# One PSUM copy for both heads, 128-column key transposes, a table row spread by TensorE, and a new order

## The chip, the core and the metric

The kernel runs on one core of a Trainium2 chip. The metric is device time in microseconds (us) of one execution; the profile of one such execution gives its span, from the first instruction to the last, and every instruction in it. Engines are TensorE (PE in the rows; PEld is its weight load), VectorE (DVE), ScalarE (ACT), GpSimd (POOL) and SyncE (SP, which here issues nearly all DMAs).

## What is computed

Attention with a learned bias by relative position, whose output goes through a feed-forward block. q, k and v are (4, 8, 576, 64), the hidden width of the bias network is 32, the feed-forward sizes are 512 and 2048, all in fp32.

```python
scores = scale * np.matmul(q, k.transpose(0, 1, 3, 2))
psi_rel = np.log1p(np.abs(rel))                       # rel[i, j] = i - j
psi_i = np.log1p(np.maximum(pos[:, None], 1.0))
x = (psi_rel / psi_i)[..., None]
h = np.maximum(x @ w1 + b1, 0.0)
bias = h @ w2                                         # one value per head
attn = softmax(scores + bias)                         # over the last axis
x = np.matmul(attn, v)                                # heads side by side: (2304, 512)
h = x @ w_in
g = h * (1.0 / (1.0 + np.exp(-1.702 * h)))
return g @ w_out
```

## The kernel before

**Tiling.** The attention is cut into units (`units`): a batch, a chunk of 128 query rows and a pair of heads. For a unit `scores` (L946) multiplies on TensorE into PSUM, `reduce` (L955, VectorE) adds the bias and takes the extreme of each row, `expo` (L964, ScalarE) takes exponentials and their row sums, `inverse` (L971, L973) inverts the sums. From the ninth unit on, the scaled exponentials are split into a high and a low 16-bit half (`exp_hi`, L991 on VectorE or L993 on ScalarE; `exp_lo`, L734 by way of `lo_part`), turned by a DMA, and multiplied with the values in `av` (L1063). The first eight units (`DIRECT = 8`) go another way: `diagonal` (L1004) makes a diagonal matrix of the inverses, `turn_pe` (L1012, L1017) turns and scales the fp32 exponentials of one head with five TensorE matmuls into the PSUM tile `op` (one bank for each head) and an `hp` tile, `turn_out` (L1022 on ScalarE, L1024 on VectorE) copies 128x512 of one head to SBUF, `turn_tail` (L1028) copies the rest, and `av_direct` (L1039) multiplies in fp32.

**Bias.** One row of distances is broadcast by a DMA to 128 partitions (`load_tab`, L580) and scaled by two engines (L569, L576). `relu` (L621 on ScalarE, L623 on VectorE) makes the hidden layer, `products` (L647) multiplies it with w2, `bias_evict` (L659, L661) leaves PSUM, and the rows go to DRAM and come back skewed, one load for each pair of heads.

**Keys.** For batches 0 and 1 (four groups of four heads) `load_k` (L798) brings a group in with one DMA, `trans_k` (L826) transposes it with 22 fp32 matmuls against the identity into the four-bank PSUM tile `sp`, ScalarE (L892) and VectorE (L734) split it. For batches 2 and 3 a DMA transposes.

**Feed-forward.** Weights come as pairs of 32-bit words of 64-bit floats; `merge` (L1197, L1201, L1205, VectorE) builds fp32, `w_split` (L1221 on ScalarE or L1223 on VectorE, then L734) makes 16-bit halves. For each of nine blocks of 256 rows and 16 slices `m1` (L1274) and `m2` (L1312) multiply; between them stand `tanh` (L1282), `gate_mul` (L1288), `gate_hi` (L1296 on ScalarE, L1298 on VectorE) and `gate_lo` (L1303, VectorE or GpSimd). `out_evict` (L1320, L1322) and `out_store` (L1332) end a block.

**Order.** Nothing in the code's sequence sets the order. Each step is a task with an engine, a duration, dependences, buffers and a priority; the class `Plan` plays the engines through and lists the tasks as they start. `TURNS` holds one priority for each task, `WHERE` names the engine of the tasks that have a choice (A ScalarE, V VectorE, P GpSimd), `SLACK` is added to each DMA's landing, `COLD` stretches TensorE's durations in a window, and `WARM` puts warming matmuls (L1369, 256 columns, output not used) ahead of numbered TensorE tasks. Every engine then runs its list strictly in that order.

## Time and profile before

| | |
|---|---|
| median of 3 runs | 656.45 us (654.28 to 656.5) |
| the profiled execution | 655.45 us |
| its span | 653.7 us |
| mean granted TensorE clock | 0.988 of full |
| busy: TensorE, VectorE, ScalarE, GpSimd | 607.3, 521.2, 370.8, 66.7 us |
| DMA | 113.91 MB, mean 174 GB/s |

A stage's busy times say which engine is full there. The chain of waits is followed back from the last instruction: each piece is the work that released the next. An engine that is full and holds most of the chain sets the stage. A granted clock of 1.00 is 2.4 GHz, 0.50 is 1.2 GHz.

### The profile page before, as it was taken

To read this page: it belongs to the slowest core of one execution; us is meant where nothing else is said; L and a number is where in the kernel's file an instruction comes from. 1 tells how busy PE (TensorE), PEld (TensorE's weight loads), DVE (VectorE), ACT (ScalarE), POOL (GpSimd) and SP (SyncE) were. 2 spreads that over 40 slices of the span, in tenths; PEclk is the share of its full clock that TensorE was granted. 3 is DMA by queue.
4 is the path that set the end of the run, shared out by engine and by line. 5 is a ranking of instruction groups with operands and counts; after the bars stand their busy time and mean duration, and the time that the engine had idled before them with its cause. 6 is when DMAs were issued, how large, how long until landed. Compare 5 with 4: busy or idle time off the path is not lost.

```text
span 653.7 us, 22298 instructions
## 1 busy us (share of the span) xinstructions
PE 607.3 (93%) x9485; PEld 433.5 (66%) x9485; DVE 521.2 (80%) x1377; ACT 370.8 (57%) x831; POOL 66.7 (10%) x101
## 2 busy tenths in 40 slices
PE   5769999988799999999899989999999999999997
PEld 2446776656565676766676657766777677767874
DVE  6996988999999979989479967977875793995322
ACT  4884577987886765556345545745434661661311
POOL 3000000121121000001011100110001200110111
PEclk9988999999999999999999989999999999999999
DMA  9997587599998799999999988979844983375000
GB/s 218 289 306 226 147 235 226 132 259 216 251 260 191 152 237 183 195 181 201 200 210 209 244 185 115 198 116 241 171 75 107 182 149 97 74 118 103 34 3 33
DMA packets 254915, 113.91 MB, mean 174 GB/s; under 512 B 233952, under 2 KB 234592, under 8 KB 254816
## 3 DMA queue, kind: packets, MB, share of 16 engines
q1 hardware_dynamic: 252192, 107.94, 78.5%
q10 hardware_dynamic: 2624, 4.55, 2.1%
q8 instruction: 74, 1.21, 0.8%
q14 instruction: 25, 0.20, 0.1%
HBM read 52.55 MB, written 15.61 MB: 104 GB/s over the span
## 4 chain that ended last, share of the span: by engine, by line
PE 63%; DVE 24%; ACT 4%; DMA 4%; issue 4%; ACTq 1%; SPq 0%; POOL 0%; DVEq 0%; POOLq 0%
PE op L1312 21%; PE hp L1274 20%; PE sp L946 6%; PE hp L1063 6%; DVE wide L734 5%; DVE wide L955 4%; PE sp L826 3%; PE op L1017 2%; DVE narrow L1201 2%; DVE th L1288 2%; DVE narrow L1205 2%; DVE w L734 2%; PE hp L1039 1%; ACT wide L964 1%; DMA wide<-in_k_dram 1%
## 5 line engine op out<-in xcount | busy, mean ns | idle before, releaser
L1274 PE MATMUL hp<-xT,w 128*64 128x256 f16 x3456 | 204.8, 273 | 4.7 <-DVE th L1288 2.8
L1312 PE MATMUL op<-w,gT 128*64 128x512 f16 x1728 | 203.2, 382 | 2.0 <-POOL gT L1303 1.3
L1274 PEld LDWEIGHTS <-w 128*64 128x64 f16 x3456 | 186.5, 110 | 24.5 <-issue 16.1
L964 ACT ACTIVATE wide<-wide,sm 128x576 f32<-128x576 f32 x144 | 110.8, 770 | 68.7 <-DVE sm L955 68.2
L1312 PEld LDWEIGHTS <-gT 128*64 128x64 f16 x1728 | 97.0, 110 | 79.5 <-issue 6.5
L1303 POOL TENSOR_TENSOR gT<-th,gT 128x256 f16<-128x256 f32 x80 | 61.7, 773 | 577.2 <-ACT gT L1296 341.9
L955 DVE CUSTOM_DVE_ANT_0 wide<-sp,wide 128x576 f32<-128x576 f32 x144 | 104.8, 752 | 7.3 <-PE sp L946 7.1
L734 DVE SCALAR_TENSOR_TENSOR wide<-wide,sm,wide 128x576 f16<-128x576 f32 x128 | 105.3, 841 | 5.2 <-ACT wide L993 4.8
L1282 ACT ACTIVATE th<-hp 128x256 f32<-128x256 f32 x144 | 53.7, 376 | 79.7 <-PE hp L1274 57.3
L1288 DVE SCALAR_TENSOR_TENSOR th<-th,hp 128x256 f32<-128x256 f32 x144 | 59.3, 416 | 48.8 <-ACT th L1282 48.2
L946 PE MATMUL sp<-wide,narrow 64*128 64x512 f16 (+2 forms) x720 | 65.5, 320 | 9.0 <-DVE sm L955 4.5
L1063 PE MATMUL hp<-wide,v 128*64 128x128 f16 (+1 forms) x2160 | 60.3, 214 | 5.0 <-issue 3.5
L1063 PEld LDWEIGHTS <-v 128*64 128x64 f16 x2160 | 57.7, 111 | 10.9 <-issue 7.0
L946 PEld LDWEIGHTS <-narrow 64*128 64x128 f16 (+1 forms) x960 | 28.8, 97 | 43.9 <-issue 23.8
L621 ACT ACTIVATE wide<-tab,bp 128x496 f32<-128x496 f32 (+17 forms) x94 | 55.4, 650 | 0.4 <-ACT narrow L1320 0.4
L993 ACT ACTIVATE wide<-wide,sm 128x576 f16<-128x576 f32 x63 | 47.2, 767 | 11.5 <-DVE sm L973 7.7
L1296 ACT CAST gT<-th 128x256 f16<-128x256 f32 x80 | 31.9, 400 | 34.7 <-DVE th L1288 21.5
L991 DVE TENSOR_SCALAR wide<-wide,sm 128x576 f16<-128x576 f32 x65 | 34.8, 545 | 0.1
L1303 DVE TENSOR_TENSOR gT<-th,gT 128x256 f16<-128x256 f32 x64 | 26.6, 422 | 4.5 <-ACT gT L1296 3.5
L971 DVE TENSOR_SCALAR sm<-sm 128x1 f32<-128x1 f32 (+1 forms) x128 | 19.9, 158 | 11.6 <-ACT wide L964 11.0
L647 PE MATMUL sp<-wide,pk 128*32 128x512 f32 (+28 forms) x312 | 23.6, 431 | 5.1 <-DVE sm L955 3.5
L964 ACT ACTIVATION_READ_ACCUMULATOR wide<-wide,sm 128x1 f32 x144 | 27.0, 188 | 0.0
(83 smaller groups left out, 513.6 us busy)
## 6 DMA issues: line engine op xcount, KB each, us to landing
wide<-scr SPq DMA_DIRECT2D x32, 576.0 KB, 4.9
scr<-narrow SPq DMA_DIRECT2D x30, 295.5 KB, 4.3
wide<-in_moe_w_in_dram SPq DMA_DIRECT2D x16, 512.0 KB, 6.0
wide<-in_moe_w_out_dram SPq DMA_DIRECT2D x16, 512.0 KB, 5.1
narrow<-in_q_dram SPq DMA_DIRECT2D x16, 256.0 KB, 4.7
out_dram<-narrow ACTq DMA_DIRECT2D x15, 256.0 KB, 2.4
w<-in_v_dram SPq DMA_DIRECT2D x4, 576.0 KB, 8.2
w<-in_k_dram SPq DMA_DIRECT2D x4, 576.0 KB, 6.3
```

What stands on the lines that cost most here:

```text
L621: nc.scalar.activation(out=h, in_=tv, func=ACTF.Relu, bias=bp[:, pb:pb + 1])
L734: nc.vector.scalar_tensor_tensor(out=out, in0=in0, scalar=scale, in1=in1, op0=ALU.mult, op1=ALU.subtract)
L946: nc.tensor.matmul(pair[64 * e:64 * e + m, a, cs], lhsT=qt[r, x, hp + e, q0:q0 + m], rhs=k_of(b, hp + e, y, cs)[r], start=i == 0, stop=i == 2,
L955: nc.vector.tensor_tensor_reduce(out=slot(("a32", u))[:, cs], in0=slot(("sp", u)).rearrange("p (h a) n -> p h (a n)", h=2)[:, a, 0:S], in1 ...
L964: nc.scalar.activation(out=t, in_=t, func=ACTF.Exp, scale=-1.0, bias=sm[:, a:a + 1], accum_out=sm[:, 2 + a:3 + a])
L993: nc.scalar.activation(out=o, in_=t, func=ACTF.Identity, scale=r)
L1063: nc.tensor.matmul(o[64 * a:64 * a + 64, po], lhsT=vt[:, x, vc:vc + 64], rhs=t[:, 9 * y + k0, po], start=kb < 0 and i == 0, stop=kb == 3 a ...
L1274: nc.tensor.matmul(p[y0:y0 + FF, :n], lhsT=wi16[:, f // 4, cc, z, w0:w0 + FF], rhs=r, start=i == 0, stop=i == 11, skip_group_check=FF < 128,)
L1282: nc.scalar.activation(out=slot(("th", j, f))[:, :n], in_=slot(("hp", j, f))[:, :n], func=ACTF.Tanh, scale=0.851 / (XS * WIS))
L1288: nc.vector.scalar_tensor_tensor(out=th, in0=th, scalar=1.0, in1=slot(("hp", j, f))[:, :n], op0=ALU.add, op1=ALU.mult)
L1303: (nc.vector if on("low", NF * j + f) == "V" else nc.gpsimd).tensor_tensor(out=gt[:, 1, :n], in0=th, in1=gt[:, 0, :n], op=ALU.subtract)
L1312: nc.tensor.matmul(o[y0:y0 + FF, i], lhsT=gt[:, z, 128 * i + y0:128 * i + y0 + FF], rhs=wo16[:, NF - 1 - f, y, :], start=f == 0 and n3 == ...
```

## The change

- `turn_out` runs once for a unit, after the second head's turning, and copies both heads' banks (128x2x512) in one instruction; `diagonal` may run on ScalarE (7 of 16 do).
- Keys of batches 0 and 1: two DMAs for a group, each partition holding four neighbouring rows, and the last 64 rows of all heads of both batches by two more DMAs, once. `trans_k` turns two heads at a time, 128 columns in one matmul, into every fourth PSUM column, and the last 64 rows in a matmul of 64 columns: 10 matmuls for 22.
- The distance row is loaded into one partition; `spread_tab` multiplies it with a column of ones into `op` (512 and 64 columns), and the two scaling instructions read it there. The inversion of the bias scale is cut into a first 32 columns and the rest.
- In the last block the second half's result goes to a bank of `sp`, and the last `m2` is cut into its halves, so that each half has its own end.
- The planner: `SLACK` 1500 in place of 2500, plus 1000 after 70 us of planned time; 4% more on VectorE, ScalarE and GpSimd after 100 us; a few durations. New `WHERE`, `TURNS` and `WARM`: 47 warming matmuls in place of 93. In instructions, VectorE's high halves of exponentials go from 65 to 48, its `gate_lo` from 64 to 51 (GpSimd's from 80 to 93), its high halves of weights from 8 to 18. `K_PE` and `Q_PE` are empty sets: their code is not reached.

```diff
-SLACK = 2500
+SLACK = 1500
 COLD = (35000, 120000, 1.1)
+LATER = (70000, 1000)
+SPARE = (100000, 1.04)
...
+                    occ = occ * (SPARE[1] if e in ("DVE", "ACT", "POOL") and now > SPARE[0] else 1)
...
-                        end += SLACK
+                        end += SLACK + (LATER[1] if now > LATER[0] else 0)
...
-        4, 21, 10, 29, 40, 28, 49, 43, 33, 68, 585, 132, 45, 705, 184, 218,
...
-    WARM = {4: 5, 9: 10, 13: 6, 14: 10, 15: 8, 16: 8, 34: 4, 39: 3, 40: 8, 46: 9, 47: 7, 53: 6, 57: 3, 59: 6}
+    WARM = {2: 10, 10: 10, 12: 5, 17: 6, 18: 6, 19: 5, 61: 5}
...
     def load_tab():
-        row = dist[0:1].rearrange("p (f a) -> p f a", f=4)[:, :, PB0:]
         nc.sync.dma_start(
-            out=slot("raw")[:, 0:S].rearrange("p (f a) -> p f a", f=4), in_=row.broadcast_to([128, 4, LPH - PB0])
+            out=slot("raw")[0:1, 0:S].rearrange("p (f a) -> p f a", f=4),
+            in_=dist[0:1].rearrange("p (f a) -> p f a", f=4)[:, :, PB0:],
         )
+    def spread_tab():
+        p = slot("tp").rearrange("p a n -> p (a n)")
+        for x, y in ((0, 512), (512, S)):
+            nc.tensor.matmul(
+                p[:, x:y], lhsT=th_tiles[0][0:1, 0:128], rhs=slot("raw")[0:1, x:y], start=True, stop=True
+            )
...
     def trans_k(b, e):
-        t, pair = slot(("k32", b, e)).rearrange("p (u k d) -> p u k d", u=2, k=9), k_psum(b, e)
+        t, pair = k_in(b, e), k_psum(b, e)
+        tail = slot(("kt", b // 2))[:, 0:512].rearrange("p (u x) -> p u x", u=NP)
         for u in range(2):
-            for c in range(5):
-                for a in range(2):
...
-                            nc.tensor.matmul(
-                                pair[64 * a:64 * a + 64, u, lo:hi], lhsT=t[po, u, 4 * a + c],
-                                rhs=idn[po, po.start + lo - x:po.start + hi - x], start=True, stop=True,
-                            )
+            for c in range(4):
+                nc.tensor.matmul(
+                    pair[:, u, c:SM:4], lhsT=t[:, u, c].rearrange("p a d -> p (a d)"), rhs=idn, start=True, stop=True,
+                )
+            nc.tensor.matmul(
+                pair[:, u, SM:S], lhsT=tail[:, 2 * e + u, :], rhs=idn[:, ST * (b % 2):ST * (b % 2) + ST],
+                start=True, stop=True,
+            )
...
-    def turn_out(u, a):
-        t = slot(("aT", u))[:, 640 * a:640 * a + 512]
-        if on("turn", 3 * u + a) == "A":
-            nc.scalar.copy(t, slot(("pt", u))[:, a])
+    def turn_out(u):
+        t = slot(("aT", u))[:, 0:512]
+        t = bass.AP(t.tensor, t.offset, [t.ap[0], (640, 2), (1, 512)])
+        if on("turn", 3 * u) == "A":
+            nc.scalar.copy(t, slot(("pt", u)))
...
+    def o_of(j, i):
+        return slot(("o2", j))[:, 0] if j == len(blocks) - 1 and i else slot(("op", j))[:, i]
...
+            for parts in [(0,), (1,)] if last and f == NF - 1 else [(0, 1)]:
```

TensorE's list, from the last bias products to the first feed-forward matmul, before (L1369 is a warming matmul, L1039 a direct product, L647 bias products, three more and six more warming matmuls stand on either side):

```order
L1369 MATMUL hp_124<-less 128x256
L1039 MATMUL hp_123<-w_63 64x128 x10
L647 MATMUL sp<-wide_95,pk 32x304 x2
L647 MATMUL sp<-wide_88,pk 32x304 x2
L647 MATMUL sp<-wide_96,pk 32x320 x2
L647 MATMUL sp<-wide_100,pk 32x320 x2
L1369 LDWEIGHTS less
```

The same place after the change (L1083 is the direct product, L666 the bias products, L1318 the first feed-forward matmul's weights):

```order
L1083 MATMUL hp_123<-w_63 64x128 x10
L1083 MATMUL hp_124<-w_63 64x128 x10
L666 MATMUL sp<-wide_88,pk 32x304 x2
L666 MATMUL sp<-wide_99,pk 32x304 x2
L666 MATMUL sp<-wide_86,pk 32x320 x2
L666 MATMUL sp<-wide_89,pk 32x320 x2
L1318 LDWEIGHTS w_63
```

The warming matmuls around the last products are gone, and two direct products stand together ahead of them.

SP's first DMAs before:

```order
L580 DMA w_63<-in_dist_dram 128x4x144
L743 DMA narrow_102<-in_q_dram 128x8x64
L903 DMA w_63<-in_v_dram 128x18x64 x2
L1190 DMA wide_84<-in_moe_w_in_dram 128x1024
L798 DMA w_63<-in_k_dram 128x18x64
```

and after (`in_dist` the distance row, `in_k` first the last 64 rows, then a group's two halves):

```order
L1234 DMA wide_84<-in_moe_w_in_dram 128x1024
L585 DMA w_63<-in_dist_dram 1x4x144
L945 DMA w_63<-in_v_dram 128x18x64
L1234 DMA wide_85<-in_moe_w_out_dram 128x1024
L1234 DMA wide_86<-in_moe_w_out_dram 128x1024
L817 DMA narrow_102<-in_k_dram 64x8x64 x2
L762 DMA narrow_104<-in_q_dram 128x8x64
L825 DMA w_63<-in_k_dram 128x8x64 x2
```

A weight load stands ahead of the distance row now, two more ahead of the first queries, which moved from second place to seventh.

ScalarE's last rows before (`narrow_108` was evicted by VectorE):

```order
L1282 ACTIVATE th_120<-hp_124 128x256
L1282 ACTIVATE th_121<-hp_123 128x256
L1296 CAST gT_118<-th_120 128x256
L1320 ACTIVATE narrow_105<-op 128x512
L1332 DMA out_dram<-narrow_108 128x512
```

and after (L1367 the two evictions, L1379 the first half's store; SP stores the second half):

```order
L1340 CAST gT_118<-th_121 128x256
L1326 ACTIVATE th_120<-hp_123 128x256
L1367 ACTIVATE narrow_105<-op 128x512
L1379 DMA out_dram<-narrow_105 128x512
L1367 ACTIVATE narrow_109<-sp 128x512
```

Both halves are ScalarE's now, from two PSUM tiles, with the first half's store between them.

## Rows read from the trace of the kernel before

**Rows 1.** Busy time of each engine by stage; first the columns, us.

```profile
core 0: us, PE busy (x) PEld busy (x) DVE busy (x) ACT busy (x) POOL busy (x), PEclk, DMA share, GB/s
0.00:47.00 47.00, 29.93 (x419) 17.68 (x419) 39.55 (x87) 32.49 (x57) 4.96 (x21) 0.97 1.01 272
47.00:117.00 70.00, 66.93 (x718) 47.78 (x719) 59.44 (x155) 45.39 (x99) 0.00 (x0) 0.94 0.75 210
117.00:205.00 88.00, 77.04 (x1170) 52.54 (x1170) 87.57 (x204) 72.98 (x166) 15.46 (x19) 1.00 0.90 218
205.00:280.00 75.00, 74.82 (x1200) 51.79 (x1198) 68.70 (x190) 46.59 (x104) 4.02 (x6) 1.00 0.98 195
280.00:380.00 100.00, 91.43 (x1780) 67.30 (x1778) 82.53 (x221) 49.69 (x119) 10.91 (x13) 1.00 1.16 208
380.00:641.00 261.00, 258.88 (x4132) 192.12 (x4130) 180.71 (x518) 122.24 (x288) 30.67 (x41) 1.00 0.62 120
641.00:653.70 12.70, 8.30 (x82) 4.33 (x78) 2.71 (x7) 1.39 (x3) 0.67 (x1) 0.94 0.12 43
```

**Rows 2.** Chain of waits by line: 60 to 117, 117 to 205, 280 to 380 us.

```profile
by line: PE op L1017 17.2%; PE hp L1039 17.2%; PE sp L826 13.0%; PE sp L946 9.1%; PE hp L1369 7.6%; DVE wide L734 5.0%; PE hp L1012 4.8%; ACT wide L964 4.6%; PE op L647 4.0%; issue 3.7%; ACT narrow L659 3.0%; ACT w L1022 2.7%; DVE wide L955
...
by line: DVE narrow L1201 12.7%; DVE wide L734 12.5%; DVE w L734 10.9%; DVE wide L955 10.5%; DVE narrow L1205 9.8%; issue 9.6%; DVE th L1288 6.5%; DVE narrow L1197 5.9%; DVE wide L623 3.4%; DVE sm L971 2.2%; DVE wide L991 2.1%; DVE xT L734 
...
by line: PE op L1312 17.9%; PE hp L1274 15.5%; PE hp L1063 8.3%; DMA wide<-in_k_dram 8.2%; DMA wide<-wide 6.6%; issue 6.4%; DMA narrow<-narrow 5.4%; DVE wide L955 4.8%; DVE wide L734 4.5%; PE sp L946 4.3%; ACT wide L964 4.0%; ACT wide L836 
```

**Rows 3.** Chain of waits, the four key transposes: start us, us, what.

```profile
17.82 3.83 PE sp L826 x42
...
47.40 6.18 PE sp L826 x39
...
69.59 3.75 PE sp L826 x42
...
88.58 3.57 PE sp L826 x39
```

**Rows 4.** TensorE alone, 38 to 55 us: us, busy, granted clock, DMA.

```profile
38.00:45.00 7.00, 3.28 (x54) 0.97 1.00 329
45.00:55.00 10.00, 8.46 (x60) 0.51 1.07 299
```

**Rows 5.** Groups by line and shape: busy us, mean ns, idle before.

```profile
L734 DVE SCALAR_TENSOR_TENSOR wide<-wide,sm,wide 128x576 f16<-128x576 f32 x128 | 105.3, 841 | 5.2 <-ACT wide L993 4.8
L955 DVE CUSTOM_DVE_ANT_0 wide<-sp,wide 128x576 f32<-128x576 f32 x144 | 104.8, 752 | 7.3 <-PE sp L946 7.1
...
L1017 PE MATMUL op<-narrow,wide 128*128 128x128 f32 x128 | 19.0, 292 | 0.0
...
L1369 PE MATMUL hp<-less 128*128 128x256 f16 x93 | 12.5, 274 | 0.8 <-ACT w L1028 0.8
...
L1022 ACT COPY w<-op 128x512 f32<-128x512 f32 x15 | 8.7, 587 | 9.4 <-PE op L1017 7.4 <-DVE w L1024 2.0
...
L892 ACT ACTIVATE wide<-sp 128x1152 f16<-128x1152 f32 x4 | 4.5, 1130 | 8.8 <-PE sp L826 8.8
```

**Rows 6.** Timeline, 0 to 8 us: start us, us, engine, line, what.

```profile
0.73 0.45 SPq L580 DMA_DIRECT2D w<-in_dist_dram  x1
...
5.38 0.46 DVE L576 TENSOR_SCALAR tab<-w,pk 128x288 f32<-128x288 f32 x1 [0.89 <-DMA w<-in_dist_dram]
...
6.26 2.21 DVE L623 TENSOR_SCALAR wide<-tab,bp 128x576 f32<-128x576 f32 x5 [0.23 <-ACT tab L569]
```

**Rows 7.** DMA issues by line: KB each, median us to landing.

```profile
wide<-in_moe_w_in_dram SPq DMA_DIRECT2D x16, 512.0 KB, 6.0
```

**Rows 8.** Timeline, the last 5 us.

```profile
649.34 0.69 DVE L1322 TENSOR_SCALAR narrow<-op 128x512 f32<-128x512 f32 x1 [3.22 <-PE op L1312]
650.07 0.60 ACT L1320 ACTIVATE narrow<-op 128x512 f32<-128x512 f32 x1 [5.72 <-DVE narrow L1322]
...
650.69 0.36 SPq L1332 DMA_DIRECT2D out_dram<-narrow  x1
```

More of the change, by code (lines that the diff above doesn't have):

```diff
@@ L649, in products_time @@
     def products_time(c, s):
-        return sum(2 * max(0.84 * (y - x), 112) for x, y, _, _ in parts_of(c, s)) + 10
+        return sum(2 * max(0.84 * (y - x), 112) for x, y, _, _ in parts_of(c, s)) + 35
     def bias_evict(c, s):
@@ L784, in add_q @@
             [tr], take=[("narrow", "qT", ("qT", b, c))], prio=p)
+        if (b, c) in Q_PE:
+            lo = add("PE", 250, lambda: nc.tensor.matmul(
+                q_psum(b, c), lhsT=less[:, 0], rhs=q_out(b, c)[:, 0], start=False, stop=True, skip_group_check=True,
+            ), [hi, t_less], prio=p)
+            qT_task[b, c] = add("ACT", act(4 * n, True), lambda: nc.scalar.activation(
+                out=q_out(b, c)[:, 1], in_=q_psum(b, c), func=ACTF.Copy, scale=QS), [lo], give=[("qp", b, c)], prio=p)
+            return
         qT_task[b, c] = add("DVE", dve(4 * n), lambda: lo_part(
@@ L797, in load_k @@
         if b // 2 not in TURNED_K:
[L798 to L801 removed]
+            for u in range(2):
+                nc.sync.dma_start(
+                    out=k_in(b, e)[:, u],
+                    in_=k[b, 4 * e + 2 * u:4 * e + 2 * u + 2, 0:SM, :].rearrange("a (p c) d -> p c a d", c=4),
+                )
             return
@@ L886, in add_k @@
             return add_turned_k(b, e)
-        p = due(first["k", b, e]) - K_LEAD
-        ld = add("SP", 350, lambda: load_k(b, e), take=[(("lateA", "lateB", "wide"), "kv", ("k32", b, e))],
-                 gate=first["k", b, e] - K_FROM, prio=p - LOAD_LEAD, dma=2600, hold=4500)
-        tr = add("PE", 2300, lambda: trans_k(b, e), [ld, t_small], take=[("s", "kp", ("kp", b, e))],
-                 give=[("k32", b, e)], prio=p)
+        p, g = due(first["k", b, e]) - K_LEAD, b // 2
+        if g not in kt_task:
+            kt_task[g] = add("SP", 700, lambda: load_kt(g), take=[("narrow", "kt", ("kt", g))],
+                             gate=first["k", b, e] - K_FROM, prio=p - LOAD_LEAD, dma=1200, n_dma=2, hold=4000)
+        ld = add("SP", 700, lambda: load_k(b, e), take=[(("lateA", "lateB", "wide"), "kv", ("k32", b, e))],
+                 gate=first["k", b, e] - K_FROM, prio=p - LOAD_LEAD, dma=2300, n_dma=2, hold=4500)
+        tr = add("PE", 1955, lambda: trans_k(b, e), [ld, kt_task[g], t_small], take=[("s", "kp", ("kp", b, e))],
+                 give=[("k32", b, e), ("kt", g)], prio=p)
         hi = add("ACT", act(2 * S, True), lambda: nc.scalar.activation(
@@ L1305, in gate_lo, with m2 @@
         )
-    def m2(j, f):
-        gt, o = slot(("gT", j, f)), slot(("op", j))
-        for i in range(blocks[j][0] // 128):
+    def o_of(j, i):
+        return slot(("o2", j))[:, 0] if j == len(blocks) - 1 and i else slot(("op", j))[:, i]
+    def m2(j, f, parts=(0, 1)):
+        gt = slot(("gT", j, f))
+        for i in parts:
             for n3, (z, y) in enumerate(((0, 0), (0, 1), (1, 0))):
@@ L1349 @@
             lo = either("low", NF * j + f, lambda j=j, f=f: gate_lo(j, f), {"V": dve(n), "P": 190 + 1.87 * n}, [hi], give=[("th", j, f)], prio=-500)
[L1350 to L1352 removed]
+            last = j == len(blocks) - 1
+            pm2s = []
+            for parts in [(0,), (1,)] if last and f == NF - 1 else [(0, 1)]:
+                pm2 = add("PE", 3 * len(parts) * 216 + 10, mode=FF_MODE, fn=lambda j=j, f=f, parts=parts: m2(j, f, parts), deps=[lo, w_task[k8 + 4 + f % 4]],
+                          after=[pm2] if pm2 else [], take=[("o", "op", ("op", j))] + [("s", "op", ("o2", j))] * last if f == 0 else [],
+                          give=[("gT", j, f)], prio=p)
+                pm2s.append(pm2)
         for i in range(n // 128):
[L1354 to L1355 removed]
+            ev = either("out", 2 * j + i, lambda j=j, i=i: out_evict(j, i), {"A": act(512, True), "V": dve(512)}, [pm2s[min(i, len(pm2s) - 1)]],
+                     take=[("narrow", "ob", ("ob", j, i))], give=[("o2" if last and i else "op", j)], prio=-600)
             add("ACT", 440, lambda j=j, i=i: out_store(j, i), [ev], give=[("ob", j, i)], prio=-700, dma=800)
```

103 lines of the change are left out of this document (56 added, 47 removed), and 327 rows, old and new, of the table TURNS.

## The prediction

> **What bounds the kernel now.** I read the busy time by stage first [rows 1], cut where the chain of waits changes its engine, then that chain stage by stage [rows 2], then single pieces of it [rows 3]. Up to 47 us no engine is full: TensorE is busy 29.93 of 47 us, and products, evictions and loads take turns. From 47 to 117 us TensorE is busy 66.93 of 70 us and VectorE 59.44; the chain of 60 to 117 us runs over TensorE's turnings (L1017 17.2%, L1039 17.2%), the key transposes (L826 13.0%) and the warming matmuls (L1369 7.6%) [rows 2]. TensorE sets this stage. From 117 to 205 us it is VectorE, 87.57 of 88 us, and nearly every large share of the chain is its own. From 205 to 641 us TensorE is full again: idle 0.18, 8.57 and 2.12 us in the three stages [rows 1]; the 8.57 lie where the DMA engines are over-subscribed (share 1.16) and the chain holds key loads, transposes and PSUM reductions [rows 2]. The last 12.70 us are the final matmuls, two evictions and two stores.
>
> So a saving counts in 47 to 117 us if it is TensorE's, in 117 to 205 us if it is VectorE's, later only if it shortens TensorE's list or fills its 10.9 us of idle, and at the very end.
>
> **The change part by part.** The sum is made against the profiled execution, 655.45 us (span 653.7, 1.75 around it); the median of the runs is 1.0 higher.
>
> *Key transposes.* Four times 22 matmuls become 8 of 128 columns and 2 of 64. On the chain they take 3.83, 6.18, 3.75 and 3.57 us [rows 3]. The nearest row for a plain fp32 matmul of 128 columns by a 128-wide weight is the turning: 128 records, two to a matmul, in 19.0 us, so 0.30 us each [rows 5]. Ten are 8 x 0.30 + 2 x 0.15 = 2.7 us. New is that they write every fourth PSUM column, which no row shows. Bounds: if that costs nothing and the weight loads hide, two thirds of 2.7, 1.8 us; if it doubles the 128-column ones, 5.1 us, worse than now. I take 2.7, the row of the same shape. The three in the TensorE stage then give 13.50 - 8.1 = 5.4 us (between +1.8 and -8.1).
>
> *Warming matmuls.* 93 become 47. Of the 93, 46 stand between 47 and 117 us; by the new order none is left between the second key transpose and the first feed-forward matmul. In 60 to 117 us they are 7.6% of the chain, 0.076 x 57 = 4.3 us. One costs 12.5 / 93 = 0.13 us [rows 5]. So TensorE's path in this stage loses 5.4 + 4.3 = 9.7 us. What is late next is VectorE: it has only 70 - 59.44 = 10.6 us of idle there [rows 1], and part of that is waiting for ScalarE, not TensorE. I let 60% through, 5.8 us; the ends are 0 and 9.7.
>
> *One copy for two heads.* Fifteen ScalarE copies and one VectorE copy of 512 become eight of 1024. A copy of 512 takes 587 ns and an eviction of 1152 takes 1130 ns [rows 5], so 1024 takes about 587 + 512 x (1130 - 587) / 640 = 1020 ns: 0.15 us of engine time less for a pair, but the direct products now wait 1.02 us after the second head's turning instead of 0.59, 0.43 us later. Behind the copy on ScalarE stand exponentials and bias evictions, so they shift too. Eight units give at most 3.5 us, none if other units' turnings cover it; the chain held this copy for 2.7% of 57 us, 1.5 us [rows 2]. I take +1.0.
>
> *Table row.* One row of 2.3 KB is loaded instead of 288 KB, and TensorE spreads it into PSUM. Before, the load left at 0.73 us, scaling began at 5.38 and the first relu at 6.26 [rows 6]. Now a weight load of 512 KB stands ahead of it on SP; such a load takes 6.0 us in the median [rows 7], so the row lands between about 3 and 7 us. The spread, 576 columns, is 4.5 times a 128-column matmul, 1.35 us. The first relu then starts 1.5 us earlier to 3 us later; VectorE also has a weight step ahead of it. I take +0.5, and -0.5 for the first key transpose (1.1 us shorter, in a stage no engine fills): 0 up to 47 us. The smaller transfer frees 288 KB at 272 GB/s [rows 1], 1 us of DMA time, and the other loads keep those engines full, so it counts as nothing.
>
> *VectorE's list in its own stage.* Where the order tells how much work stands ahead of the 28th gate product (about the end of this stage), I counted rows and priced them by the durations of before: VectorE has 4 more score reductions (752 ns) and 3 more low halves (841 ns) done by then [rows 5], 5.5 us; it gives away 6 bias evictions, 12 value splits and 7 diagonals and takes 10 weight halves more, and its list is 1.7 us longer in all. That leaves it 3.8 us ahead at equal work. ScalarE pays for it with some 9 us more by the same point, on top of 72.98 of 88 us [rows 1]. I take -2, ends 0 and -4.
>
> *Later.* Over the run VectorE loses 17 high halves of exponentials to ScalarE and 13 low halves of the gate to GpSimd. Neither is the limit after 205 us. TensorE's list there is the same, so only its 10.9 us of idle can move; a new order may leave anything from none to twice that. I take -1, ends -8 and +8. The margins themselves issue nothing.
>
> *End.* Now VectorE evicts half 0 from 649.34, ScalarE half 1 from 650.07, and the last store leaves at 650.69 [rows 8]. The second eviction waits for the first although its own data are there. After the change half 0 is evicted under the last six matmuls and half 1 (0.60) right behind them: 0.7 us less. If the store of half 0, issued ahead on the same engine, is in the way, 0.3 us less.
>
> Sum: 0 - 5.8 + 1.0 - 2 - 1 - 0.7 = -8.5; 655.45 - 8.5 = 647.0 us.
>
> **Clock.** TensorE ran at 0.51 of full rate (the 1.2 GHz level) from 45 to 55 us, after being busy only 3.28 of 7 us [rows 4]; the transpose at 47.40 took 6.18 us there, 3.75 at full clock [rows 3]. The change takes warming matmuls away just ahead of that place: between the first two scores there were 32, now 12. From 60 to 117 us the clock held with TensorE busy nearly throughout [rows 1], so I expect the same short dip. The Trainium skill ("TensorE: Matmul & The Clock Gate", section "HAM oscillation — how this bites in real kernels") says that idle gaps between matmul bursts put the clock back to its lower level. By that rule the removal itself costs clock, and the time is that of the first rival. The trace agrees as far as the one dip goes.
>
> **Rivals.**
> 1. *The clock stays low (slower).* Fewer warming matmuls leave TensorE at half rate well past 55 us. Busy time at half rate costs its half: 8.46 us of it cost about 4.2 [rows 4]. The gain of 8.5 is gone once TensorE spends 17 us more of busy time at half rate than today; with 24 us, a third of the stage, it is +12 on its path while the 5.8 still passes: 655.45 + 12 - 5.8 = 661.7. For it: the dip of today sits there. Against: the stage is dense, and the shorter transposes bring work closer together.
> 2. *VectorE and ScalarE take TensorE's place at once (no change).* If the waits in 47 to 117 us alternate so closely that removing TensorE work only lengthens its idle, the 5.8 and the 2 vanish: 655.45 + 1.0 - 0.7 - 1 = 654.8. For it: VectorE has 85% there, ScalarE 65%, and ScalarE's share grows.
> 3. *All of it passes (much faster).* 9.7 through, copies hidden, VectorE 4 ahead, most of the 8.57 us of idle at 280 to 380 us gone: 655.45 - 9.7 - 4 - 7 - 0.7 = 634. For it: VectorE's total is smaller and the attention runs further ahead.
> 4. *A load is late early (about no change).* The planner's allowance for a landing falls from 2500 to 1500 ns before 70 us, and a transpose now waits for three loads where it waited for one. With the DMA engines full (1.01) up to 47 us [rows 1], one load late by 5 to 9 us stops TensorE's queue with products and scores behind it: 652 to 656.
>
> **How the numbers follow.** My forecast, 640 to 653, has 0.60; rival 3 0.12, rival 2 0.10, rival 4 0.06, rival 1 0.12. The range leaves about a tenth on either side: rival 3's far end below 637, and rival 1 at its price above 661. It also takes in the bounds of the parts (-8 to +8 for the late idle being the widest). Within 0.5% is 653.2 to 659.7, about what a measurement of this kernel can tell from no change. Faster: 0.60 + 0.12 less a little, 0.71; same: rival 2 and most of rival 4, 0.14; slower: rival 1 and the rest, 0.15.
>
> **What would show it.** In the changed profile: each group of key transposes about 2.7 us; fewer than 10 us at the lower clock; the first feed-forward matmul, at the head of the 117 us stage now, near 112; VectorE full from there to about 197 us; TensorE idle of about 10 us between 205 us and the end; the last store 0.7 us closer to the last matmul. I am wrong if the clock row stays at 0.5 past 60 us, if VectorE's idle before 117 us stays at 10 us or more, or if TensorE's idle after 205 us goes over 18 us.

## The result, and the profile after

The changed kernel takes 646.28 us in the median (644.3 to 647.6), the kernel before beside it 655.37 (653.06 to 656.5). The ratio is 0.9863, 95% interval 0.9821 to 0.9905: faster by 1.4%. 647.0 was predicted. The profiled execution took 647.09 us, 645.3 of them its span, so it is 8.4 us shorter in span than the one of before.

Busy time by stage of the changed kernel answers [rows 1] (start:end, us; then busy us and count of TensorE, its weight loads, VectorE, ScalarE, GpSimd; granted clock; DMA share; GB/s):

```profile
0.00:47.00 47.00, 31.58 (x377) 19.21 (x378) 37.22 (x82) 35.37 (x63) 4.85 (x22) 0.96 0.97 257
47.00:117.00 70.00, 63.30 (x700) 47.26 (x701) 64.81 (x165) 48.67 (x104) 1.75 (x2) 0.98 0.84 228
117.00:205.00 88.00, 76.56 (x1164) 51.15 (x1158) 82.69 (x200) 73.26 (x164) 13.03 (x16) 0.98 0.96 219
205.00:280.00 75.00, 74.13 (x1167) 49.57 (x1164) 65.25 (x181) 52.55 (x114) 9.77 (x13) 1.00 0.99 192
280.00:380.00 100.00, 93.87 (x1818) 69.61 (x1812) 79.72 (x214) 45.89 (x110) 9.57 (x12) 1.00 1.09 205
380.00:633.00 253.00, 252.90 (x4046) 186.59 (x4044) 181.03 (x506) 120.81 (x285) 36.82 (x50) 1.00 0.64 122
633.00:645.30 12.30, 8.30 (x102) 5.35 (x98) 1.98 (x5) 2.37 (x5) 0.16 (x1) 0.94 0.12 44
```

From 47 to 117 us TensorE is busy 3.6 us less and idle 6.70 us in place of 3.07, while VectorE rose from 59.44 to 64.81: the two have come close to each other. From 117 to 205 us VectorE, full before, is idle 5.3 us. The chain of waits says the same, for 60 to 117 us and 117 to 205 us, against [rows 2]:

```profile
by line: DVE wide L997 14.0%; DMA wide<-in_moe_w_out_dram 10.9%; PE op L1060 9.9%; DVE narrow L1245 9.6%; DVE narrow L1249 8.3%; PE hp L1083 7.4%; DVE narrow L1241 5.0%; DVE wide L753 4.6%; DVE w L753 4.6%; issue 4.3%; PE hp L1055 3.1%; DVE
...
by line: DMA wide<-scr 13.9%; DVE wide L997 13.0%; DVE wide L753 8.3%; DVE narrow L1249 7.7%; DVE narrow L1245 6.7%; DMA narrow<-in_q_dram 6.3%; DVE w L753 4.8%; issue 4.0%; DVE narrow L1241 3.6%; DVE th L1332 3.4%; PE hp L1318 3.1%; ACT wi
```

TensorE's turnings (L1060, L1083 now) went from 17.2% each to 9.9% and 7.4%, key transposes and warming matmuls left the head of the list, and the score reduction (L997) and the weight merges (L1241 to L1249) of VectorE took their place, with one weight load. In the second stage two kinds of load stand among VectorE's steps that weren't there before.

How far the kernel is at an instant can be read from steps that both orders have. In the timelines, these are the first feed-forward matmul, the score reductions with numbers 20, 40 and 143 (counted from 0; 143 is the last one) and the 28th gate product, a step of the feed-forward. They stand in order of time, first before:

```profile
117.54 1.50 PE L1274 MATMUL hp<-xT,w 128*64 128x256 f16 x24
...
121.75 0.76 DVE L955 CUSTOM_DVE_ANT_0 wide<-sp,wide 128x576 f32<-128x576 f32 x1
...
204.57 0.76 DVE L955 CUSTOM_DVE_ANT_0 wide<-sp,wide 128x576 f32<-128x576 f32 x1
...
234.75 0.42 DVE L1288 SCALAR_TENSOR_TENSOR th<-th,hp 128x256 f32<-128x256 f32 x1
...
586.25 0.74 DVE L955 CUSTOM_DVE_ANT_0 wide<-sp,wide 128x576 f32<-128x576 f32 x1
```

and after:

```profile
110.32 2.81 PE L1318 MATMUL hp<-xT,w 128*64 128x256 f16 x48
...
123.28 0.75 DVE L997 CUSTOM_DVE_ANT_0 wide<-sp,wide 128x576 f32<-128x576 f32 x1
...
197.69 0.76 DVE L997 CUSTOM_DVE_ANT_0 wide<-sp,wide 128x576 f32<-128x576 f32 x1 [0.75 <-DMA wide<-wide]
...
239.35 0.41 DVE L1332 SCALAR_TENSOR_TENSOR th<-th,hp 128x256 f32<-128x256 f32 x1
...
578.30 0.75 DVE L997 CUSTOM_DVE_ANT_0 wide<-sp,wide 128x576 f32<-128x576 f32 x1
```

The lead is 7.2 us at the first feed-forward matmul, 6.9 at reduction 40 and 7.9 at the last one, but reduction 20 comes 1.5 us later than before and the 28th gate product 4.6 us later. The new order sets attention and feed-forward differently against each other, so no single step tells where the time was won.

TensorE's rows tell more, because the span is its busy time and its idle time. Summed over the stages, before and after, it is busy 607.3 and 600.6 us (6.7 less), idle up to 205 us 31.1 and 33.6 us (2.5 more), and idle from 205 us to the end 15.3 and 11.1 us (4.2 less). Of the 8.4 us, about half is thus work that TensorE no longer does, less the idle time that came in its place before 205 us, and half is idle time that went after 205 us. The prediction had 6.8 of its 8.5 us won before 205 us.

### The profile page after: what moved, and what is told of

Read it like the earlier page. It is cut to its first block, busy times and chain, and to the rows that moved or that the text cites. A ratio compares the mean times of both kernels' runs of the same rounds, so it can differ in the third digit from the quotient of the medians.

```text
span 645.3 us, 22079 instructions
## 1 busy us (share of the span) xinstructions
PE 600.6 (93%) x9347; PEld 428.7 (66%) x9347; DVE 512.7 (79%) x1348; ACT 378.9 (59%) x841; POOL 75.9 (12%) x115
## 4 chain that ended last, share of the span: by engine, by line
PE 67%; DVE 18%; DMA 6%; ACT 4%; issue 2%; SPq 2%; ACTq 0%; DVEq 0%
PE hp L1318 24%; PE op L1359 23%; PE hp L1107 7%; PE sp L988 6%; DVE wide L997 4%; DMA wide<-scr 3%; DVE narrow L1245 2%; DVE wide L753 2%; DVE narrow L1249 2%; PE sp L666 2%; PE sp L1359 2%; DVE w L753 1%; DVE wide L642 1%; DVE narrow L1241 1%; ACT wide L640 1%
## 5 line engine op out<-in xcount | busy, mean ns | idle before, releaser
L1318 PE MATMUL hp<-xT,w 128*64 128x256 f16 x3456 | 206.4, 274 | 2.9 <-DVE th L1332 2.0
L1318 PEld LDWEIGHTS <-w 128*64 128x64 f16 x3456 | 187.2, 110 | 23.9 <-issue 13.7
L1359 PE MATMUL op<-w,gT 128*64 128x512 f16 x1632 | 194.2, 380 | 4.5 <-DVE gT L1347 1.9
L1359 PEld LDWEIGHTS <-gT 128*64 128x64 f16 x1728 | 95.1, 110 | 84.7 <-issue 6.9
L1347 POOL TENSOR_TENSOR gT<-th,gT 128x256 f16<-128x256 f32 x93 | 71.1, 766 | 555.9 <-ACT gT L1340 255.5
L997 DVE CUSTOM_DVE_ANT_0 wide<-sp,wide 128x576 f32<-128x576 f32 x144 | 104.5, 750 | 10.9 <-PE sp L988 5.7
L1035 ACT ACTIVATE wide<-wide,sm 128x576 f16<-128x576 f32 x80 | 59.6, 767 | 8.5 <-DVE sm L1015 6.3
L640 ACT ACTIVATE wide<-tab,bp 128x480 f32<-128x480 f32 (+16 forms) x91 | 54.6, 652 | 0.6 <-DVE tab L582 0.6
L1340 ACT CAST gT<-th 128x256 f16<-128x256 f32 x76 | 30.3, 401 | 31.1 <-DVE th L1332 19.8
L1342 DVE CAST gT<-th 128x256 f16<-128x256 f32 x68 | 20.5, 303 | 11.3 <-PE op L1359 5.4
L1347 DVE TENSOR_TENSOR gT<-th,gT 128x256 f16<-128x256 f32 x51 | 21.4, 420 | 9.2 <-ACT gT L1340 8.0
L1033 DVE TENSOR_SCALAR wide<-wide,sm 128x576 f16<-128x576 f32 x48 | 27.8, 585 | 0.4
L666 PE MATMUL sp<-wide,pk 128*32 128x79 f32 (+26 forms) x288 | 23.1, 449 | 5.1 <-DVE sm L997 3.5
```

The source lines that it names most:

```text
L640: nc.scalar.activation(out=h, in_=tv, func=ACTF.Relu, bias=bp[:, pb:pb + 1])
L997: nc.vector.tensor_tensor_reduce(out=slot(("a32", u))[:, cs], in0=slot(("sp", u)).rearrange("p (h a) n -> p h (a n)", h=2)[:, a, 0:S], in1 ...
L1035: nc.scalar.activation(out=o, in_=t, func=ACTF.Identity, scale=r)
L1318: nc.tensor.matmul(p[y0:y0 + FF, :n], lhsT=wi16[:, f // 4, cc, z, w0:w0 + FF], rhs=r, start=i == 0, stop=i == 11, skip_group_check=FF < 128,)
L1347: (nc.vector if on("low", NF * j + f) == "V" else nc.gpsimd).tensor_tensor(out=gt[:, 1, :n], in0=th, in1=gt[:, 0, :n], op=ALU.subtract)
L1359: nc.tensor.matmul(o_of(j, i)[y0:y0 + FF], lhsT=gt[:, z, 128 * i + y0:128 * i + y0 + FF], rhs=wo16[:, NF - 1 - f, y, :], start=f == 0 and ...
```

## The experiments

Three theories. **A**: TensorE sets 47 to 117 us, and some 60% of the work taken from it reaches the end. **B**: VectorE, ScalarE and the loads set that stretch, and the gain is the new order's. **C**: the warming matmuls late in that stage held the clock, and taking them out costs clock. Each ratio is to runs of the kernel before on the same chip. One execution of a kernel lies up to 5 us from the median, so a difference of a few us between two traces decides nothing by itself; a lead that builds up step by step between two kernels of one order is another matter.

### e1: before, without the late warming matmuls

```diff
-    WARM = {4: 5, 9: 10, 13: 6, 14: 10, 15: 8, 16: 8, 34: 4, 39: 3, 40: 8, 46: 9, 47: 7, 53: 6, 57: 3, 59: 6}
+    WARM = {4: 5, 9: 10, 13: 6, 14: 10, 15: 8, 16: 8}
```

> The kernel before with the 46 warming matmuls that stand after 47 us taken out; its order is untouched. Theory A (TensorE sets 47 to 117 us, and 60% of what is taken off its list there reaches the end): 46 x 0.134 us are 6.2 us, 4.3 of them on the chain, so 2.6 us less, 652.8 beside 655.4, ratio 0.996. Theory B (the work in that stage is bounded by VectorE, ScalarE and loads, and the gain of the change is that of its new order): no change, 655.4, and TensorE's idle between 47 and 117 us grows from 3.1 to about 9 us. Theory C (the late warming matmuls hold the clock): a second stretch at the lower clock after 60 us and 2 us or more longer.

0.9953 (0.9927 to 0.9979), 3.1 us faster. Reduction 20, at 121.75 us before, starts at 119.64. So in the old order the warming matmuls cost time on TensorE's path and their absence costs no clock that shows. A fits here, C falls.

### e2: e1 with fewer matmuls in a key group

Eighteen matmuls a group in place of 22 (36 records in place of 44; the fourteen below is a miscount). Some write the wrong columns, so the scores of batches 0 and 1 are other numbers; the work around them is the same.

```diff
+            for x, n in ((64, 128), (192, 128), (320, 128), (448, 64)):
+                nc.tensor.matmul(
+                    pair[:, u, x:x + n], lhsT=t[:, u, x // 128:x // 128 + 2].rearrange("p k d -> p (k d)"), rhs=idn[:, 0:n],
+                    start=True, stop=True,
+                )
-            for c in range(5):
+            for c in (0, 4):
```

> The same, and each group of key transposes of the kernel before with 14 matmuls in place of 22 (the inner columns of two heads in one matmul of 128 columns, from wrong rows, so the scores of batches 0 and 1 are not the reference's; loads, order and everything else as before). A group should take about 2.7 us at full clock where it took 3.75. Theory A: 60% of 6.2 + 4 x 1.05 on top of the first theory's number, in all 5 us less, 650.4, ratio 0.992. Theory B: 655 and more idle on TensorE.

0.999 (0.9959 to 1.0022): no gain. This says nothing against A, because the groups didn't become shorter. The third group of e1, at full clock, and the first and last rows of the same group in e2:

```profile
69.45 3.82 PE L826 MATMUL sp<-idn,w 128*64 128x128 f32 x44
...
71.72 1.00 PE L820 MATMUL sp<-idn,w 128*128 128x128 f32 x8
...
74.68 1.07 PE L831 MATMUL sp<-idn,w 128*64 128x128 f32 x10
```

That is 3.82 us and, from 71.72 to 75.75, 4.03 us, where 2.7 were expected. Whether shorter key groups alone help the old order stays untested. By the medians e2 is slower than e1, and its trace has two other things that go with it. First the clock, 45 to 65 us in e2 (clock in the third place from the end; from 35 to 45 us it is 1.00):

```profile
45.00:55.00 10.00, 8.46 (x51) 6.31 (x48) 5.77 (x17) 3.03 (x8) 0.00 (x0) 0.50 1.01 273
55.00:65.00 10.00, 9.21 (x74) 6.81 (x74) 7.02 (x18) 4.84 (x10) 0.00 (x0) 0.82 0.64 177
```

and in e1, 35 to 65 us:

```profile
35.00:45.00 10.00, 7.28 (x96) 4.41 (x95) 9.97 (x23) 8.49 (x18) 0.00 (x0) 0.86 1.08 331
45.00:55.00 10.00, 8.46 (x67) 6.21 (x63) 6.49 (x18) 4.64 (x9) 0.00 (x0) 0.67 0.97 268
55.00:65.00 10.00, 8.92 (x97) 6.24 (x98) 8.59 (x24) 5.58 (x13) 0.00 (x0) 0.96 0.71 211
```

Half rate is 0.50, so of TensorE's busy time 8.46 + 0.36 x 9.21 = 11.8 us ran at it in e2 and 0.28 x 7.28 + 0.66 x 8.46 + 0.08 x 8.92 = 8.3 in e1 ([rows 4] show the same place before). Busy time at half rate costs its half, so e2 lost 1.7 us there. Then a weight load (`in_moe_w_in`, 8.5% of 60 to 117 us, 4.8 us) stands in e2's chain of waits, and none in e1's. Reduction 20 starts 2.8 us behind e1's.

### e3 and e4: after, with the late warming matmuls back, and with none

```diff
-    WARM = {2: 10, 10: 10, 12: 5, 17: 6, 18: 6, 19: 5, 61: 5}
+    WARM = {2: 10, 10: 10, 12: 5, 17: 6, 18: 6, 19: 5, 34: 4, 39: 3, 40: 8, 46: 9, 47: 7, 53: 6, 57: 3, 59: 6, 61: 5}
```

> The changed kernel with 41 of the taken warming matmuls put back between the second key transposes and the first feed-forward matmul, at the same numbers of TensorE's tasks as before; order untouched. Theory A: 5.5 us more TensorE work, 3 to 4 us longer, 649.8 beside 646.3. Theory B: they fall into TensorE's idle there (6.7 us between 47 and 117 us), 646.3, and the idle falls to about 2 us.

0.9867 (0.9824 to 0.9909), by the medians the same as the changed kernel, though the two intervals leave room for 3 us. In e3's trace the first feed-forward matmul starts at 111.93 us, 1.6 later than in the changed kernel, and the last matmul ends at the same instant (641.33 against 641.30). What cost 3.1 us in the old order leaves no cost that shows in the new one.

```diff
-    WARM = {2: 10, 10: 10, 12: 5, 17: 6, 18: 6, 19: 5, 61: 5}
+    WARM = {}
```

> The changed kernel with no warming matmul at all. If the lower clock matters: longer stretches at half rate between 28 and 80 us (they cover about 4 and 4 us now) and 3 to 6 us longer, 650 to 652. If the stage up to 117 us is not TensorE's any more: within 1.5 us of 646.3.

0.9839 (0.9787 to 0.9891): the same or a little faster. With no warming matmul at all, the first two stages read

```profile
0.00:47.00 47.00, 26.01 (x340) 15.65 (x341) 36.91 (x80) 35.00 (x63) 4.85 (x22) 0.93 0.96 256
47.00:117.00 70.00, 62.45 (x717) 46.53 (x718) 67.13 (x172) 49.37 (x106) 1.75 (x2) 1.00 0.82 234
```

TensorE is idle 7.55 us of the 70 and its granted clock is 1.00 throughout. That ends theory C and the prediction's first rival for the new order. The Trainium skill ("TensorE: Matmul & The Clock Gate", section "HAM oscillation — how this bites in real kernels") says that idle gaps between bursts put the clock back. The trace agrees ahead of 47 us, where the mean clock is 0.93, and shows nothing of it in the stage from which the warming matmuls were taken.

### e5 and e6: the parts without the order, the order without the parts

Every task of the changed kernel is there, but emitted in the sequence of the kernel before, with its engines and buffers; new tasks stand where what they replace stood, the warming is e1's, and the last rows of the keys lie in a buffer that is still free then.

```diff
-        plan.order()
+        plan.seq = [plan.tasks[i] for i in [
...
+        plan.env = {
...
-        return tiles[pool][i]
+        return tiles[pool][i].bitcast(F32) if key == ("kt", 0) else tiles[pool][i]
```

> The changed kernel's instructions (short key transposes, one copy, table row by TensorE, split last block) emitted in the order of the kernel before, engine by engine, with the six early warming groups of e1. Compare with e1 (0.9953). Theory A (TensorE's removed work in 47-117 us reaches the end): 5.4 us less of key work at 60 % and 0.3 at the end: about 3.5 us under e1, ratio 0.990. Theory B (VectorE, ScalarE and loads set that stretch; the gain is the new order's): as e1, 0.994 to 0.997, with TensorE's work in 47-117 us down by 3 to 5 us and its idle time there up by as much.

0.9882 (0.9837 to 0.9927), 4.7 us faster than e1. A's 0.990 is inside, and the chain of 60 to 117 us is VectorE's now, as B said of the new order alone:

```profile
by line: DVE wide L997 14.8%; DVE narrow L1245 12.4%; DVE w L753 11.4%; DVE narrow L1249 11.1%; DVE wide L753 7.1%; issue 6.1%; DVE narrow L1241 6.1%; ACT wide L1006 5.6%; DVE wide L642 4.5%; DVE v L753 3.1%; DVE narrow L1050 3.1%; DVE xT L
```

In e1 the same line begins with L1017, the keys (L826) and L1039, 40.2% together. The lead on e1 is 1.3 us at the first reduction, 2.7 at number 8 and 5.0 at number 20, then most of it stays (3.9 at number 40, 5.4 at the last).

The other half is the kernel before with its own instructions in the sequence of the changed kernel, the two copies at the place of the one:

```diff
-        plan.order()
+        plan.seq = [plan.tasks[i] for i in [
...
+        plan.env = {
...
-    WARM = {4: 5, 9: 10, 13: 6, 14: 10, 15: 8, 16: 8, 34: 4, 39: 3, 40: 8, 46: 9, 47: 7, 53: 6, 57: 3, 59: 6}
+    WARM = {1: 10, 9: 10, 11: 5, 16: 6, 17: 6, 18: 5, 60: 5}
```

> The instructions of the kernel before (22 key transposes a group, two copies, the table row by a broadcast DMA, whole last block) emitted in the order of the changed kernel, with its engine choices, its slots and its few warming matmuls. Theory A: the key work comes back (5.4 us, 60 % of it, so +3.2), the two copies +1: about 0.991 to 0.993. Theory B: the order keeps nearly the whole gain, 0.985 to 0.989; it may even be faster, since the table is ready at 5.4 us and not at 9.2.

0.9896 (0.9861 to 0.9931). By the medians the order alone is worth 3.7 us against e1, the parts alone 4.7, both together 5.9 (0.9863 against 0.9953). Each brings a large part of the gain by itself. A fits the old order (e1, e5) and B the new one (e3 above, e8 below), so neither is right alone. The intervals, 2 to 3 us on each, would still allow that the two simply add: an overlap isn't shown by these ratios, and only e3 and e8 speak for it.

### e7 and e8: two copies again, more key work, both in the changed kernel

```diff
-            nc.scalar.copy(t, slot(("pt", u)))
+            for x in range(2):
+                nc.scalar.copy(t[:, x], slot(("pt", u))[:, x])
```

> The changed kernel with two copies of 512 columns in place of the one of 1024, one after the other on the engine that has the one now. From the trace of the kernel before, one copy of 512 on ScalarE is about 0.59 us, so 1.18 in place of 1.01: eight times 0.17 = 1.4 us more of ScalarE and VectorE work. Theory A: within 0.1 % of the changed kernel (0.986). Theory B: up to 0.2 % slower (0.988) where the copy's engine is the late one. The prediction charged the one copy with +1.0 us for coming later; this run doesn't undo that wait, only the size.

0.9836 (0.9798 to 0.9875), no loss. The pair takes 1.16 us (14 of 582 ns), the one copy 1.01.

```diff
         for u in range(2):
-            for c in range(4):
+            for c in (0, 1, 2, 3, 0, 1, 2, 3) if u else range(4):
```

> The changed kernel with four of each key group's eight strided transposes done twice: about 1.1 us more of TensorE work in each of four groups between 29 and 90 us, 4.5 us in all. Theory A: 60 % of it reaches the end, +2.7 us, 0.990. Theory B: under 1 us, 0.986 to 0.987, TensorE's work in 47-117 us up by about 2 to 4 us and its idle time there down by as much.

0.9829 (0.9788 to 0.987), no loss, and A's 0.990 lies outside. The four doubled matmuls took 0.89 us a group, not the 1.1 I had written:

```profile
68.92 1.16 PE L848 MATMUL sp<-idn,w 128*128 128x128 f32 x8
...
70.08 2.00 PE L848 MATMUL sp<-idn,w 128*128 128x128 f32 x16
```

and the stage reads

```profile
47.00:117.00 70.00, 65.93 (x746) 49.49 (x746) 66.87 (x171) 49.32 (x105) 1.75 (x2) 1.00 0.85 234
```

TensorE's busy time in the stage rose by 2.6 us, from 63.30 to 65.93, and its idle time fell by as much: B, for the new order. TensorE has room there, and the key work isn't what sets the stage any more.

### e9 and e10: which part carries it in the old order

e1 with the one copy, where the second of the two stood:

```diff
-    def turn_out(u, a):
-        t = slot(("aT", u))[:, 640 * a:640 * a + 512]
+    def turn_out(u):
+        t = slot(("aT", u))[:, 0:512]
+        t = bass.AP(t.tensor, t.offset, [t.ap[0], (640, 2), (1, 512)])
```

> e1 (the kernel before with only its six early warming groups) with one change: both heads' turned exponentials in one copy of 1024 columns where the second of the two copies stood. e5 minus e1 is about 5 us by the twentieth score sum. Theory A1 (the key transposes carry that gain): as e1, ratio 0.995, and no milestone earlier by over 1 us. Theory A2 (the one copy carries it): 0.988 to 0.990, milestones 3 to 5 us earlier by the twentieth score sum. My prediction's charge of +1.0 us for the later copy would show as 0.9965.

0.9957 (0.993 to 0.9985), as e1 by the medians. Its reduction 20 starts at 118.70, 0.9 us ahead of e1, although the low clock lasted longer:

```profile
35.00:45.00 10.00, 6.29 (x92) 3.74 (x84) 9.76 (x21) 8.01 (x17) 0.00 (x0) 0.90 1.05 336
45.00:55.00 10.00, 8.46 (x58) 6.50 (x54) 5.26 (x16) 3.91 (x7) 0.00 (x0) 0.50 1.09 276
55.00:65.00 10.00, 8.79 (x90) 6.17 (x90) 8.30 (x21) 4.32 (x10) 0.00 (x0) 0.91 0.55 171
```

0.20 x 6.29 + 8.46 + 0.18 x 8.79 = 11.3 us of busy time at half rate against e1's 8.3, which cost it 1.5. By the medians the charge of +1.0 us for the later copy isn't seen, but 0.9965 lies inside this interval too, so e9 doesn't decide on it.

e10 is e5 with the two copies back at their old places:

```diff
-    def turn_out(u):
-        t = slot(("aT", u))[:, 0:512]
-        t = bass.AP(t.tensor, t.offset, [t.ap[0], (640, 2), (1, 512)])
+    def turn_out(u, a):
+        t = slot(("aT", u))[:, 640 * a:640 * a + 512]
```

> e5 (the changed kernel's instructions in the old order) with one change: the two copies of 512 columns at their old places. Theory A1 (keys): as e5, 0.988. Theory A2 (one copy): back to e1's 0.995, with the milestones of e1. If each carries a part, both this and e9 lie between 0.990 and 0.993.

0.9931 (0.9905 to 0.9957), between e1 and e5. Reduction 20 of the five kernels in the old order, from their timelines:

| | start of reduction 20, us | median ratio |
|---|---|---|
| before | 121.75 | 1 |
| e1, no late warming | 119.64 | 0.9953 |
| e9, and one copy | 118.70 | 0.9957 |
| e10, and the other parts, two copies | 116.10 | 0.9931 |
| e5, all parts | 114.67 | 0.9882 |

The traces give warming 2.1 us, the keys and the other parts 3.5, the copy 0.9 to 1.4. The medians put less on the keys (1.4) and more on the copy (3.2, beside nothing in e9). How the 4.7 us divide is open. That the one copy doesn't cost the +1.0 us there is shown only narrowly: e5 lies 0.0049 under e10, with about 0.005 to either side, where the charge would put it 0.0015 above.

### e11 and e12: the start and the tail

In the changed kernel the start went wrong (below). e11 puts the row's load first on SP's queue and the first weight load behind the first value load, VectorE's first steps in the order of need, and the last block's first store on SP. It has no warming matmuls, as e4.

```diff
+        move(t_row, 0)
+        move(first_w, pos(v1) + 1)
...
-            q_ = nc.sync if j == len(blocks) - 1 and off else nc.scalar
+            q_ = nc.sync if j == len(blocks) - 1 else nc.scalar
```

> The changed kernel without its seven groups of warming matmuls (as e4), with the table row's and the scalars' loads ahead of the first weight load on SyncE's queue, VectorE's first steps in the order of need (the first 32 columns of the scaled bias, then the tables, the other 112 columns and the first weight merge behind the fifth relu), and the last block's first store issued by SyncE in place of ScalarE. From e4's trace: the first relu on VectorE at 10.93 us would come at about 7 us, 3 to 4 us earlier. If the start reaches the end, 1 to 3 us under e4; if VectorE's total work up to 117 us sets it, nothing. The store saves the 0.41 us that the second half's eviction stands behind the store's issue. In all: ratio 0.979 to 0.984 against e4's 0.9839.

0.9871 (0.9841 to 0.9901): no gain. The start of TensorE and GpSimd's setup in e11:

```profile
2.81 0.35 PE L603 MATMUL hp<-pk,one 128*32 128x36 f32 x8 [2.81 <-DMA pk<-in_pack_dram]
6.21 2.39 PE L596 MATMUL op<-w,th 1*128 1x512 f32 x4 [3.05 <-POOL th L591]
...
5.96 0.19 POOL L591 MEMSET th<- 1x128 f32 x1
```

The scalars were there at 2.8 us, 3.0 earlier than in e4, but the spread (L596) stayed at 6.21: it waits for the column of ones, whose memset (L591) is the last step of GpSimd's setup. The tail did what was expected of it: half 1's eviction starts at 644.02, 0.04 us behind the last matmul, and the span ends 3.6 us behind that matmul instead of 4.0.

e12 is e11 with that memset first on GpSimd's queue and VectorE's second reciprocal ahead of the tables.

```diff
+        move(t_ones, 0)
```

> e11 showed that the table row's spread (6.21 us) didn't wait for the row or the scalars, which were there at 2.7 us, but for the memset of the ones, which stands last in GpSimd's setup (5.96 us, 0.19 us long). This run is e11 with that memset first on GpSimd's queue, and VectorE's reciprocal of the other 112 columns ahead of the tables, in the idle time there. If the start was held by that memset: spread at 3.1 to 3.6 us, first relu on VectorE at 6.5 to 7.2 (9.72 in e11, 10.93 in e4), first score sum 2 to 4 us earlier than e11's 46.8. If the start reaches the end: 1 to 3 us under e4, ratio 0.979 to 0.983; if VectorE's work up to 117 us sets the stage, the lead is given back by the twentieth score sum (122.7 us in e11, 121.4 in e4), ratio 0.984 to 0.987.

0.9847 (0.9808 to 0.9886), as e4. The start came forward as expected:

```profile
3.08 2.39 PE L596 MATMUL op<-w,th 1*128 1x512 f32 x4
...
6.59 2.20 DVE L642 TENSOR_SCALAR wide<-tab,bp 128x576 f32<-128x576 f32 x5
```

and the chain of waits of its first 47 us:

```profile
by line: DMA w<-in_v_dram 18.5%; SPq L825 10.7%; SPq L1234 9.3%; PE sp L848 8.0%; ACT wide L640 7.4%; ACT v L958 7.3%; DVE wide L642 4.1%; SPq L817 3.6%; ACT wide L1006 3.0%; DVE w L753 2.9%; DVE wide L753 2.9%; issue 2.9%; DVE narrow L1245
```

The first relu on VectorE is 4.3 us ahead of e4's (10.93), the first reduction 1.3 us (44.57 against 45.87), reduction 20 none (122.00 against 121.36). The chain goes over a value load and SP's issues now: the relu wasn't what the first scores wait for. No version that I ran beats the changed kernel by more than these intervals.

## Why the prediction was right, point by point

| term | predicted, us | measured, us |
|---|---|---|
| 0 to 47 us | 0 | e12 wins 4.3 at the first relu, nothing at reduction 20 |
| 47 to 117 us: keys and warming, and the copy | -5.8 + 1.0 | -7.2 at the first feed-forward matmul, +1.5 at reduction 20; by the parts alone in the old order -7.1 (e5 against before, reduction 20) |
| VectorE's stage | -2 | not seen: VectorE is idle 5.3 us there, the 28th gate product comes 4.6 later |
| later, TensorE's idle up to the last stage | -1 | -3.8 (10.87 to 7.10) |
| end | -0.7 | -0.4 |
| sum | -8.5 | -8.4 (span) |

The measured column doesn't add up to the span, since its steps measure different work. The forecast of the sum was right, and its closeness is partly luck: the VectorE term didn't come, the late term was too small by nearly 3 us, and the two errors nearly cancel.

**Key transposes.** A group at full clock takes 2.4 us, predicted 2.7 (the second group; the first one fell into the dip of the clock and took 4.1):

```profile
50.38 1.16 PE L848 MATMUL sp<-idn,w 128*128 128x128 f32 x8
51.37 0.33 PE L851 MATMUL sp<-idn,narrow 128*128 128x64 f32 x2
51.54 1.11 PE L848 MATMUL sp<-idn,w 128*128 128x128 f32 x8
52.49 0.33 PE L851 MATMUL sp<-idn,narrow 128*128 128x64 f32 x2
```

Writing every fourth PSUM column costs nothing that can be seen. The last three groups take 2.44, 2.42 and 2.34 us where [rows 3] had 13.50 together: 6.3 us less, 5.4 predicted. 2.5 of the 6.3 are the clock, since the group of 6.18 us now runs outside the dip.

**Warming and the share that passes.** The mechanism fits the order of before: e1 and e5 take 2.1 and 5.0 us off the way to reduction 20, 7.1 together, more than the 60% of 9.7 that I let through. In the kernel as it stands it isn't borne out: there VectorE has the largest shares of the chain, and e3 and e8 show no loss when TensorE work is put back. VectorE's idle time before 117 us is 5.2 us, under the 10 that would have proved the prediction wrong.

**One copy.** The size was right (1020 ns worked out from [rows 5], 1.01 us measured). The step that fails is the charge of 0.43 us a unit for the products' longer wait: e9 can't tell it from nothing, and e5 against e10 speaks for a gain. The prediction had named the reason itself, that other units' turnings may cover the wait; no run here shows that this is what happens.

**VectorE's own stage.** The -2 didn't come. The 28th gate product, up to which I had counted VectorE's rows as about the end of this stage, stands at 234.75 us, 30 us behind it, in a stage where TensorE is full. Up to that point the counts are right, but the changed kernel reaches it later. VectorE, busy 87.57 of 88 us before [rows 1], is busy 82.69 and waits for the rest, for ScalarE and for loads in about equal parts: the danger that my fourth rival put ahead of 47 us and which arises here. SyncE's queue from 183 us on, and the reduction that waits:

```profile
183.00 0.58 SPq L735 DMA_DIRECT2D wide<-scr  x1
183.69 6.03 SPq L1092 DMA_TRANSPOSE wide<-wide  x1
189.82 0.53 SPq L735 DMA_DIRECT2D wide<-scr  x1
...
189.73 0.76 DVE L997 CUSTOM_DVE_ANT_0 wide<-sp,wide 128x576 f32<-128x576 f32 x1 [0.71 <-DMA wide<-scr]
```

A bias load leaves at 183.00 and lands 6.6 us later, and the next is held behind a DMA transpose that occupies the queue for 6.03 us. This is read from the trace; moving the loads ahead wasn't tried.

**Later, and the end.** TensorE's idle time from 205 us to the end is 11.1 us (0.87, 6.13, 0.10 and 4.00 in the rows), about 10 predicted, 15.3 before. Of this the late term, -1, was sized too small. Up to the last stage TensorE idles 7.1 us there in place of 10.9, and the new order goes with it: from 205 us to the last matmul TensorE idles 4.8 to 9.9 us (6.6 in the mean) in the eight traces with the new order, e6 among them with 8.9, and 8.7 to 12.6 us (11.0 in the mean) in the six with the old one. From 380 us on it is 0.1 to 0.2 us in all eight, 0.9 to 4.8 in all six. Which of the order's moves does it wasn't tried. At the end the saving is the smaller of the two that I had named, because, unlike in [rows 8], the store of half 0 stands between the two evictions on ScalarE:

```profile
640.48 0.81 PE L1359 MATMUL sp<-w,gT 128*64 128x512 f16 x6
...
640.69 0.60 ACT L1367 ACTIVATE narrow<-op 128x512 f32<-128x512 f32 x1 [4.09 <-PE op L1359]
641.32 0.34 ACTq L1379 DMA_DIRECT2D out_dram<-narrow  x1
641.70 0.60 ACT L1367 ACTIVATE narrow<-sp 128x512 f32<-128x512 f32 x1 [0.41 <-PE sp L1359]
```

The last matmul ends at 641.29, half 1's eviction starts 0.41 us later. e11 takes the store away, and the 0.41 with it.

**Start.** The prediction's bounds (the first relu 1.5 us earlier to 3 later) were too narrow: it is at 10.98, 4.7 us later than in [rows 6]. I had looked for the row's landing alone, and taken a full-clock price for the spread; the spread waits for the memset of the ones (e11), takes 2.39 us and not 1.35, the scalars land at 5.87, and two weight steps stand ahead on VectorE. It did no harm, for the reason that I gave: no engine is full there, and other waits end later (e12).

**The first rival.** 3.06 + 3.44 = 6.5 us of TensorE's busy time ran at half rate by the clock row (in 29 to 33 and 77 to 81 us, 0.57 each), under the 8.3 of before; with a third dip at 162.5 to 166 us (0.51, busy throughout) it is 9.9, just under the 10 predicted. e4 excludes the mechanism for this order. e2 and e9 show only what a longer dip costs in the old one, 1.5 to 1.7 us for 3.0 to 3.5 us of busy time: they have the six early warming groups that e1 and the kernel before have, so their dips don't come from fewer of them.
